# Keys of both branches in three single PSUM banks per tile, and a third row tile transposed on the array

## The chip, the cores and the metric

The kernel runs on one core of a Trainium2 chip. The metric is the device time of one execution in microseconds, and smaller is better.

## The reference

The reference computes two linear-attention branches, A and B, on the same input rows and mixes them with a gate. For `x` of 2048 rows by 640 columns and each branch with its own `wqkv` (640 x 1920) and `wo` (640 x 640):

```
qkv = (x @ wqkv) split into q, k, v with H = 32 heads of 20
phi = lambda t: where(t > 0, t + 1, exp(t)) + 1e-6
pq, pk = phi(q), phi(k)
kv = einsum("bhsd,bhse->bhde", pk, v);   z = einsum("bhsd->bhd", pk)
o  = einsum("bhqd,bhde->bhqe", pq, kv) / (einsum("bhqd,bhd->bhq", pq, z) + 1e-6)
branch = o (heads joined) @ wo
g = sigmoid(sum(x * gate_w))          # one number per row
result = g * branch_A + (1 - g) * branch_B
```

All operands are bfloat16. `phi` is computed as max(t, 0) + (min(exp(t), 1) + 1e-6), which is the same function.

## The kernel before

The 2048 rows are 16 row tiles of 128 (`NT`), and the 640 input columns are five chunks of 128 (`NC`). `XT` holds x transposed (chunk columns on the partitions, rows along the free side), which is the stationary operand of the key products; `XN` holds x as it is.

There are four stages in the order of TensorE. First the keys of both branches for all 16 tiles. Then, for each branch, five sums over all rows of keys times x (`g_unit`, L643 and L644), with the query products (`q_unit`, L797) between them. Then small products for the key-value matrices (L705, whose moving operand takes five runs of 24 columns) and for those times `wo` (L740). Last, the output products (L957), which ScalarE and VectorE bring out of PSUM.

Every operation is recorded by a helper with an estimated cost, the buffers that it reads and writes, and a priority. A planner then runs the list in simulated time. TensorE keeps the order in which its work was recorded; ScalarE (ACT), VectorE (DVE) and SyncE (SP) take the operation that can start earliest. From this come the final order on each engine, the PSUM banks, and the semaphore waits. PSUM is a pool of 8 banks of 512 fp32 columns; a buffer takes one bank, or two neighbouring ones. The loads at the beginning are chained by queue in the order recorded.

The loads go out from SP (L354 in the trace, the helper's line) in this order: x tile 0, then the five weight chunks of A's keys (called A0 to A4 below) and the five of B's (B0 to B4), 160 KB each. Then seven transposing DMAs bring the row tiles 2 to 15 into `XT` (the first four take one tile each), one plain load brings x rows 256 to 2047 into `XN`, and last come the other weights. x tile 1 and the gate weights are issued from ACT's queue.

Tiles 0 and 1 don't wait for transposing DMAs. `x_tp` (L479) multiplies each plain 128 x 128 block of x by the identity `IDN` on TensorE, which transposes it into PSUM, and three copies (L496, one block, two blocks, two blocks) bring it into `XT`: on VectorE for tile 0, on ScalarE for tile 1. While their weights come in, A's keys of tiles 0 and 1 are interleaved chunk by chunk. `gate_col` puts the gate weights into the column after B's key weights (a small matmul at L516 and a copy at L519), so that column 640 of B's key product is the gate's logit.

A key product of one tile and one branch (`k_step`) is five steps, one for each chunk, and each step is a matmul of 512 columns (L535) and one of 128 (A) or 129 columns (B, L536) into a buffer of two PSUM banks. `k_post` then runs: for B a one-column exponential for the gate (L561), an exponential over 640 columns on ACT into a slot of `EK` (L568), a clamp in place on DVE (L571), and the sum with max(t, 0) on DVE, which reads PSUM (L579) and writes the keys `PK`. `EK` has four slots of 640 columns, one for each product. The query exponentials (L814) wait for the last key of branch B, since their slots lie over `EK`.

`warm` (L466) is work for TensorE before data is there. The lines around the start read:

Of the kernel before, what the change touches and what calls it, by code (L numbers as in the profile page):

```python
# [7 lines left out]
ALU = mybir.AluOpType  # L8
# [3 lines left out]
D = 640  # L12
# [64 lines left out]
class Sched:  # L77
# [187 lines left out]
def body(nc, A_x, A_wqkv, A_wo, B_x, B_wqkv, B_wo, gate_w, out, log=None):  # L265
# [9 lines left out]
    XT = sb("XT", [128, NC, S], bf)  # L275
    XN = sb("XN", [128, NT, XS_W], bf)
    WKW = sb("WKW", [128, 2 * NU * D], bf)
    WK = {
        "A": WKW[:, 0 : NC * D].rearrange("p (c f) -> p c f", c=NC),
        "B": WKW[:, NC * D : NC * (D + KB_W)].rearrange("p (c f) -> p c f", c=NC),  # L280
    }
    WQ = {X: sb("WQ" + X, [128, NC, D], bf) for X in XS}
    WV = {X: sb("WV" + X, [128, NC, D + 8], bf) for X in XS}
    WO = {X: sb("WO" + X, [128, NU, D], bf) for X in XS}
    PK = {X: sb("PK" + X, [128, NT * D], bf) for X in XS}
    PKt = {X: PK[X][:, :].rearrange("p (t f) -> p t f", t=NT) for X in XS}
    EX = [sb("EX%d" % i, [128, NC, 512], bf) for i in range(3)]

    def slot(X, i):
# [58 lines left out]
    def dma(q, name, dst, src, nbytes, ins=(), outs=(), after=(), issue=450.0, transpose=False, prio=None):  # L348
        timing = (330.0, 1500.0) if not transpose else (140.0, 1500.0) if loading else (1000.0, 1150.0)

        def fn(e):
            d = dst() if callable(dst) else dst
            with nc.allow_non_contiguous_dma(reason="layout"):
                return e.dma_start(d, src() if callable(src) else src, transpose=transpose)  # L354

        o = op(q, fn, 0.0, ins, outs, after, prio=prio, name=name, dma=(issue, nbytes) + timing)
        if loading:
            o.behind = chain.get(q)
            chain[q] = o
        return o  # L360
# [4 lines left out]
    def act_cost(n):  # L365
        return 190 + 0.833 * n

    def dve1(n):
        return 155 + 1.04 * n
# [34 lines left out]
    def ld_x(q, t):  # L404
        dma(q, "x%d" % t, XN[:, t, 0:D], x[128 * t : 128 * t + 128, :], 163840, outs=[bxn[t]])

    def ld_wk(q, X, c, after=()):
        dma(q, "wk%s%d" % (X, c), WK[X][:, c, 0:D], wqkv[X][128 * c : 128 * c + 128, D : 2 * D], 163840, outs=[bwk[X, c]], after=after)
# [19 lines left out]
    for c in range(NC):  # L428
        if c == 0:
            ld_x("SP", c)  # L430
        ld_wk("SP", "A", c)
    for c in range(NC):
        ld_wk("SP", "B", c)
    for t0, t1 in ((2, 3), (3, 4), (4, 5), (5, 6), (6, 8), (8, 12), (12, 16)):
        xt_dma(t0, t1)
    dma("SP", "xr", XN[:, 2:NT, 0:D], x[256:S, :].rearrange("(t p) d -> p t d", p=128), 14 * 163840, outs=bxn[2:])
    for X in XS:
        dma("SP", "wq" + X, WQ[X][:, :, :], w3(X, 0), 819200, outs=[bwq[X]])
    for X in XS:
# [22 lines left out]
    def warm(n, w=4):  # L462
        for i in range(n):
            op(
                "PE",
                lambda e: e.matmul(psw(bw, 128 * w), ONE[:, 0:1].to_broadcast([128, 128]), ONE[:, 0:1].to_broadcast([128, 128 * w]), start=True, stop=True),  # L466
                107.0 * w,
                ins=[bone],
                outs=[bw],
                name="warm",  # L470
            )

    def x_tp(t):
        for lo, hi in ((0, 1), (1, 3), (3, 5)):
            bt = Buf("tp", "ps")
            for c in range(lo, hi):
                op(
                    "PE",
                    lambda e, c=c, lo=lo, bt=bt: e.matmul(  # L479
                        PS[:, bt.slot, 128 * (c - lo) : 128 * (c - lo) + 128],  # L480
                        XN[:, t, 128 * c : 128 * c + 128],
                        IDN[:, :],
                        start=True,
                        stop=True,
                    ),
                    100.0,
                    ins=[bxn[t], bid],
                    outs=[bt],
                    name="tp%d" % t,
                )  # L490
            half = Buf("xth")

            def copy(e, lo=lo, hi=hi, bt=bt):
                o = XT[:, lo:hi, 128 * t : 128 * t + 128]
                i = PS[:, bt.slot, 0 : 128 * (hi - lo)].rearrange("p (c s) -> p c s", c=hi - lo)
                return e.activation(o, i, ACT.Copy) if t else e.tensor_copy(o, i)  # L496

            op(
                "ACT" if t else "DVE",
                copy,  # L500
                act_cost(128 * (hi - lo)) if t else dve1(128 * (hi - lo)),
                ins=[bt],
                outs=[half],
                name="tpc%d" % t,
            )
            bxt[t].parts = getattr(bxt[t], "parts", []) + [half] * (hi - lo)
# [3 lines left out]
    def gate_col():  # L510
        bt = Buf("gwp", "ps")

        def tv():
            return PS[:, bt.slot, 0:NC]

        op("PE", lambda e: e.matmul(tv(), GWZ[:, :], IDN[:, 0:NC], start=True, stop=True), 60.0, ins=[bgw, bid], outs=[bt], name="gwt")  # L516
        op(
            "DVE",
            lambda e: e.tensor_copy(WK["B"][:, :, D : D + 1], tv().unsqueeze(2)),  # L519
            170.0,  # L520
            ins=[bt],
            outs=[bgc],
            name="gwc",
        )
# [4 lines left out]
    def k_step(X, t, c, ps):  # L529
        w = D + 1 if X == "B" else D  # L530

        def fn(e):
            a = psw(ps, w)
            l = XT[:, c, 128 * t : 128 * t + 128]
            e.matmul(a[:, 0:512], l, WK[X][:, c, 0:512], start=(c == 0), stop=(c == NC - 1))  # L535
            return e.matmul(a[:, 512:w], l, WK[X][:, c, 512:w], start=(c == 0), stop=(c == NC - 1))  # L536

        xin = [bxt[t].parts[c] if hasattr(bxt[t], "parts") else bxt[t]]
        op(
            "PE",  # L540
            fn,
            mm_cost(512) + mm_cost(128),
            ins=xin + [bwk[X, c]] + ([bgc] if X == "B" else []),
            outs=[ps],
            name="k%s%d_%d" % (X, t, c),
        )
# [3 lines left out]
    def k_post(X, t, ps):  # L550
        ek = Buf("ek", "ek")
        ek2 = Buf("ek2")
        pk = Buf("pk%s%d" % (X, t))
        bpk[X, t] = pk
        first = []
        if X == "B":
            b = Buf("ge")
            bge.append(b)
            op(
                "ACT",  # L560
                lambda e: e.activation(GE[:, t : t + 1], psw(ps, D + 1)[:, D : D + 1], ACT.Exp, scale=-1.0),  # L561
                200.0,
                ins=[ps],
                outs=[b],
                name="ge",
            )
            first = [b]
        op("ACT", lambda e: e.activation(EK[:, ek.slot, :], psw(ps, D), ACT.Exp), act_cost(D), ins=[ps] + first, outs=[ek], name="ke")  # L568
        op(
            "DVE",  # L570
            lambda e: e.tensor_scalar(EK[:, ek.slot, :], EK[:, ek.slot, :], 1.0, EPS, op0=ALU.min, op1=ALU.add),  # L571
            dve4(D),
            ins=[ek],
            outs=[ek2],
            name="kt",
        )
        op(
            "DVE",
            lambda e: e.scalar_tensor_tensor(PKt[X][:, t, :], psw(ps, D), 0.0, EK[:, ek.slot, :], op0=ALU.max, op1=ALU.add),  # L579
            dve1(D),  # L580
            ins=[ps, ek, ek2],
            outs=[pk],
            name="ks",
        )

    def k_unit(X, t):
        ps = Buf("k", "ps", 2)
        for c in range(NC):
            k_step(X, t, c, ps)
        k_post(X, t, ps)  # L590

    warm(4)
    warm(1, 2)
    pss = [Buf("k", "ps", 2) for _ in range(2)]
    x_tp(0)
    warm(1, 1)
    x_tp(1)
    for c in range(2):
        for t in range(2):
            k_step("A", t, c, pss[t])  # L600
    gate_col()
    for c in range(2, NC):
        for t in range(2):
            k_step("A", t, c, pss[t])
    for t in range(2):
        k_post("A", t, pss[t])
    pss = [Buf("k", "ps", 2) for _ in range(2)]
    for c in range(NC):
        for t in range(2):
            k_step("B", t, c, pss[t])  # L610
    for t in range(2):
        k_post("B", t, pss[t])
    for t in range(2, NT):
        for X in XS:
            k_unit(X, t)

    LOW = 10**6

# [529 lines left out]
```

## Time and profile before

| | us |
|---|---|
| median of 4 runs | 188.0 |
| lowest, highest | 187.92, 188.52 |
| profiled execution, own time | 188.52 |
| its span, first to last instruction | 186.8 |
| TensorE busy in the span | 183.4 |
| ScalarE busy | 94.8 |
| VectorE busy | 136.9 |

The profiled execution is the slowest of the four runs, and its span leaves 1.72 us that lie around the instructions. The TensorE clock was granted in full (1.000) over the whole span.

Busy time of the engines in stretches of the span, in us:

| stretch | work of TensorE | PE | DVE | ACT |
|---|---|---|---|---|
| 0 to 7.65 | first loads, transposes, A's keys of tiles 0 and 1 | 6.37 | 1.21 | 2.43 |
| 7.65 to 48.6 | all other keys | 40.95 | 34.21 | 24.00 |
| 48.6 to 100 | sums over rows, queries | 51.40 | 31.96 | 28.66 |
| 100 to 150 | the rest of them, small products, first outputs | 49.99 | 46.79 | 31.19 |
| 150 to 186.8 | outputs | 34.73 | 22.68 | 8.55 |

A line for a group of instructions names the source line, the engine, the operation, what is written from what, the shape and the count; then the busy time of all, the printed nanoseconds of one, and the time in which the engine sat idle ahead of them with what ended it. Matmuls overlap in the pipeline, so the printed length of one is longer than the distance from its start to the next one's. PEld is the loading of the stationary operand, which runs beside the matmuls. A line of a timeline gives the start, the length, the engine, the source line and the operation.

### The profile page before, as it was taken

How to read it: one execution, taken by the hardware profiler on the slowest of the kernel's cores; microseconds unless marked ns; L12 is line 12 of the kernel's file. 1: busy time of each engine (PE TensorE's matmuls, PEld its weight loads, DVE VectorE, ACT ScalarE, POOL GpSimd, SP SyncE). 2: the span in 40 equal slices, each digit the busy share in tenths (PEclk: the TensorE clock that was granted, in tenths of full speed). 3: DMA queues.
4: the chain of work that ended last, by engine and by line, in shares of the span. 5: the costliest groups of instructions: out<-in, count | busy, mean ns of one | idle time of the engine just before them, and what ended most of it. 6: DMA issues, size and time to landing. Idle time of an engine off the chain costs nothing.

```text
span 186.8 us, 3272 instructions
## 1 busy us (share of the span) xinstructions
PE 183.4 (98%) x1297; PEld 106.6 (57%) x1297; DVE 136.9 (73%) x264; ACT 94.8 (51%) x167; POOL 0.8 (0%) x10
## 2 busy tenths in 40 slices
PE   8899999999999999999999999999999999999995
PEld 4455555555555655555557555555567555555553
DVE  2289888888833455487699999998799996359653
ACT  5265655656454546544675566788623784400001
POOL 1000000000000000000000000000000000000000
PEclk9999999999999999999999999999999999999999
DMA  7989999997001011010611312116515346613434
GB/s 193 290 156 142 211 387 368 364 213 154 4 0 35 0 39 35 0 35 10 85 28 35 74 28 51 28 41 174 177 35 115 64 100 168 171 70 108 142 106 140
DMA packets 36501, 21.38 MB, mean 114 GB/s; under 512 B 25694, under 2 KB 36230, under 8 KB 36486
## 3 DMA queue, kind: packets, MB, share of 16 engines
q1 hardware_dynamic: 36188, 20.97, 45.1%
q8 instruction: 10, 0.16, 0.4%
q10 hardware_dynamic: 298, 0.20, 0.3%
q14 instruction: 5, 0.04, 0.1%
HBM read 10.87 MB, written 4.26 MB: 81 GB/s over the span
## 4 chain that ended last, share of the span: by engine, by line
PE 96%; DMA 2%; SPq 1%; DVE 0%; issue 0%; DVEq 0%
PE ps L957 23%; PE ps L797 23%; PE ps L643 18%; PE ps L535 18%; PE ps L644 5%; PE ps L536 5%; DMA WKW<-in_A_wqkv_dram 2%; PE ps L705 2%; PE ps L740 1%; SPq L354 1%; DVE TSB L1001 0%; DVEq L237 0%
## 5 line engine op out<-in xcount | busy, mean ns | idle before, releaser
L535 PE MATMUL ps<-WKW,XT 128*128 128x512 bf16 x160 | 43.9, 380 | 0.8 <-DMA WKW<-in_A_wqkv_dram 0.8
L814 ACT ACTIVATE EK<-ps 128x512 bf16<-128x512 f32 x40 | 23.9, 598 | 30.7 <-PE ps L797 30.6
L536 PE MATMUL ps<-WKW,XT 128*128 128x128 bf16 (+1 forms) x160 | 35.1, 220 | 0.0
L568 ACT ACTIVATE EK<-ps 128x640 bf16<-128x640 f32 x32 | 22.3, 704 | 10.4 <-PE ps L536 5.0
L535 PEld LDWEIGHTS ps<-WKW,XT 128*128 128x128 bf16 x160 | 15.7, 98 | 19.8 <-DMA WKW<-in_A_wqkv_dram 1.2
L797 PE MATMUL ps<-XT,WQA 128*128 128x512 bf16 x100 | 24.5, 379 | 0.0
L797 PE MATMUL ps<-XT,WQB 128*128 128x512 bf16 x100 | 23.8, 380 | 0.0
L643 PE MATMUL ps<-XN,PKB 128*128 128x512 bf16 x80 | 23.5, 379 | 0.0
L643 PE MATMUL ps<-XN,PKA 128*128 128x512 bf16 x80 | 23.5, 379 | 0.0
L824 DVE TENSOR_SCALAR EK<-EK 128x512 bf16<-128x512 bf16 x40 | 11.5, 288 | 13.7 <-ACT EK L814 13.7
L644 PE MATMUL ps<-XN,PKA 128*128 128x129 bf16 x80 | 17.6, 220 | 0.0
L644 PE MATMUL ps<-XN,PKB 128*128 128x129 bf16 x80 | 17.6, 220 | 0.0
L957 PE MATMUL ps<-WPA,EX 128*128 128x512 bf16 x120 | 17.0, 299 | 0.0
L957 PE MATMUL ps<-WPB,PKA 128*128 128x512 bf16 x120 | 16.5, 299 | 0.0
L797 PEld LDWEIGHTS ps<-XT,WQB 128*128 128x128 bf16 x100 | 10.9, 118 | 8.8 <-issue 0.4
L571 DVE TENSOR_SCALAR EK<-EK 128x640 bf16<-128x640 bf16 x32 | 10.4, 325 | 7.4 <-ACT EK L568 7.3
L536 PEld LDWEIGHTS ps<-WKW,XT 128*128 128x128 bf16 x160 | 15.7, 98 | 0.0
L797 PEld LDWEIGHTS ps<-XT,WQA 128*128 128x128 bf16 x100 | 10.6, 117 | 8.1
L643 PEld LDWEIGHTS ps<-XN,PKA 128*128 128x128 bf16 x80 | 9.4, 117 | 7.9
L643 PEld LDWEIGHTS ps<-XN,PKB 128*128 128x128 bf16 x80 | 9.4, 117 | 7.9
L579 DVE SCALAR_TENSOR_TENSOR PKB<-ps,EK 128x640 bf16<-128x640 f32 x16 | 13.2, 825 | 0.6
L579 DVE SCALAR_TENSOR_TENSOR PKA<-ps,EK 128x640 bf16<-128x640 f32 x16 | 13.2, 825 | 0.6
(77 smaller groups left out, 222.3 us busy)
## 6 DMA issues: line engine op xcount, KB each, us to landing
out_dram<-TSB SPq DMA_DIRECT2D x15, 160.0 KB, 1.8
XN<-in_A_x_dram SPq DMA_DIRECT2D x1, 2240.0 KB, 9.2
WKW<-in_A_wqkv_dram SPq DMA_DIRECT2D x5, 160.0 KB, 4.4
WKW<-in_B_wqkv_dram SPq DMA_DIRECT2D x5, 160.0 KB, 4.3
WQA<-in_A_wqkv_dram SPq DMA_DIRECT2D x1, 800.0 KB, 10.8
WQB<-in_B_wqkv_dram SPq DMA_DIRECT2D x1, 800.0 KB, 13.4
WVA<-in_A_wqkv_dram SPq DMA_DIRECT2D x1, 800.0 KB, 12.7
WVB<-in_B_wqkv_dram SPq DMA_DIRECT2D x1, 800.0 KB, 14.4
```

Of the source, the lines that this page charges most:

```text
L535: e.matmul(a[:, 0:512], l, WK[X][:, c, 0:512], start=(c == 0), stop=(c == NC - 1))
L536: return e.matmul(a[:, 512:w], l, WK[X][:, c, 512:w], start=(c == 0), stop=(c == NC - 1))
L568: op("ACT", lambda e: e.activation(EK[:, ek.slot, :], psw(ps, D), ACT.Exp), act_cost(D), ins=[ps] + first, outs=[ek], name="ke")
L571: lambda e: e.tensor_scalar(EK[:, ek.slot, :], EK[:, ek.slot, :], 1.0, EPS, op0=ALU.min, op1=ALU.add),
L579: lambda e: e.scalar_tensor_tensor(PKt[X][:, t, :], psw(ps, D), 0.0, EK[:, ek.slot, :], op0=ALU.max, op1=ALU.add),
L643: e.matmul(a[:, 0:512], l, XN[:, t, 0:512], start=(t == 0), stop=(t == NT - 1))
L644: return e.matmul(a[:, 512 : D + 1], l, XN[:, t, 512 : D + 1], start=(t == 0), stop=(t == NT - 1))
L705: r = e.matmul(PS[0:n, ps.slot, GR * i : GR * i + NC * w], WV[X][:, c, lo : lo + n], gv[:, c, :, 24 * u : 24 * u + w], start=(c == 0), sto ...
L797: r = e.matmul(PS[:, ps.slot, :], WQ[X][:, c, g::5], XT[:, c, 512 * b : 512 * b + 512], start=(c == 0), stop=(c == NC - 1),)
L814: lambda e: e.activation(EQ[:, eq.slot, :], PS[:, ps.slot, :], ACT.Exp),
L824: lambda e: e.tensor_scalar(EQ[:, eq.slot, :], EQ[:, eq.slot, :], 1.0, EPS, op0=ALU.min, op1=ALU.add),
L957: r = e.matmul(a[:, l0 - lo : h0 - lo], PQ[X, b][:, g, 128 * (t % 4) : 128 * (t % 4) + 128], WP[X][:, g, l0:h0], start=(X == first and g = ...
```

## The change

Two things change, both in the key stage.

The head: row tile 2 is no longer brought by a transposing DMA. It is loaded plainly, from SP after the first A weight chunk, and transposed on TensorE by `x_tp(2)` with its three copies on VectorE. The bulk load into `XN` begins at row 384. A's keys of tiles 0, 1 and 2 are then interleaved as the weights come in, and B's keys of these three tiles follow tile by tile with `k_unit`.

From tile 3 on, a new function `k_both` takes the place of the two `k_unit` calls. The 640 + 640 key columns and the gate column of one tile are computed as three products in single banks: 512 columns of A, then 258 columns (129 of A and 129 of B in one matmul, whose moving operand is two runs), then 512 columns of B. The weights of both branches lie beside each other in `WKC` for this, and the gate column is written behind both. The exponentials, clamps and sums follow the banks: exponentials of 512, 256 and 512 columns and the gate's one, one clamp over 768 columns and one over 512, sums of 512, 256 and 512. `EK` serves as two pairs of slots, one pair for a tile. `PK` of both branches is one tensor now, so that one sum can write both.

```diff
+    WKC = WKW[:, 0 : NC * 2 * KB_W].rearrange("p (c x f) -> p c x f", c=NC, x=2)
+    WK = {X: WKC[:, :, i, :] for i, X in enumerate(XS)}
...
+    PKS = sb("PKS", [128, 2, NT * D], bf)
+    PK = {X: PKS[:, i, :] for i, X in enumerate(XS)}
...
         ld_wk("SP", "A", c)
+        if c == 0:
+            ld_x("SP", 2)
     for c in range(NC):
         ld_wk("SP", "B", c)
-    for t0, t1 in ((2, 3), (3, 4), (4, 5), (5, 6), (6, 8), (8, 12), (12, 16)):
+    for t0, t1 in ((3, 4), (4, 5), (5, 6), (6, 8), (8, 12), (12, 16)):
         xt_dma(t0, t1)
...
-                "ACT" if t else "DVE",
+                "ACT" if t == 1 else "DVE",
                 copy,
...
-            lambda e: e.tensor_copy(WK["B"][:, :, D : D + 1], tv().unsqueeze(2)),
+            lambda e: e.tensor_copy(WKC[:, :, :, D : D + 1], tv().unsqueeze(2).unsqueeze(3).to_broadcast([128, NC, 2, 1])),
...
+    def k_both(t):
+
+        ps = [Buf("k", "ps") for _ in range(3)]
+        ek = Buf("ek", "ek", 2, (0, 2))
...
+        for i in range(3):
+
+            def fn(e, i=i):
+                for c in range(NC):
+                    r = WKC[:, c, :, 512 : D + 1] if i == 1 else WKC[:, c, i // 2, 0:512]
+                    x = e.matmul(two() if i == 1 else bank(i), XT[:, c, 128 * t : 128 * t + 128], r, start=(c == 0), stop=(c == NC - 1))
+                return x
...
+        op("ACT", lambda e: e.activation(ekw(0, 512), bank(0), ACT.Exp), act_cost(512), ins=[ps[0]], outs=[ek, ea], name="ke")
+        op("ACT", lambda e: e.activation(GE[:, t : t + 1], two()[:, 0, D - 512 : D - 511], ACT.Exp, scale=-1.0), 200.0, ins=[ps[1]], outs=[b], name="ge")
+        op(
+            "ACT",
+            lambda e: e.activation(ekw(512, 768).rearrange("p (x f) -> p x f", x=2), two()[:, :, 0:128], ACT.Exp),
...
+        clamp(0, 768, [ea, em], ta)
+        add(PKt["A"][:, t, 0:512], lambda: bank(0), lambda: ekw(0, 512), 0, [ta], [pk["A"]])
+        add(
+            PKS[:, :, D * t + 512 : D * t + D],
...
+        op("ACT", lambda e: e.activation(ekw(768, 1280), bank(2), ACT.Exp), act_cost(512), ins=[ps[2]], outs=[ek, eb], name="ke")
+        clamp(768, 1280, [eb], tb)
+        add(PKt["B"][:, t, 0:512], lambda: bank(2), lambda: ekw(768, 1280), 2, [tb], [pk["B"]])
...
     warm(1, 1)
     x_tp(1)
+    for t in range(2):
+        k_step("A", t, 0, pss[t])
+    x_tp(2)
+    for t in range(2):
+        k_step("A", t, 1, pss[t])
     for c in range(2):
-        for t in range(2):
-            k_step("A", t, c, pss[t])
+        k_step("A", 2, c, pss[2])
     gate_col()
-    for c in range(2, NC):
+    for c in range(2, 4):
         for t in range(2):
             k_step("A", t, c, pss[t])
     for t in range(2):
+        k_step("A", t, 4, pss[t])
         k_post("A", t, pss[t])
...
+    for c in range(2, NC):
+        k_step("A", 2, c, pss[2])
+    k_post("A", 2, pss[2])
+    for t in range(3):
+        k_unit("B", t)
+    for t in range(3, NT):
+        k_both(t)
```

More of the change, by code (lines that the diff above doesn't have):

```diff
@@ L277, in body @@
     WKW = sb("WKW", [128, 2 * NU * D], bf)
[L278 to L281, printed above, removed]
+    WKC = WKW[:, 0 : NC * 2 * KB_W].rearrange("p (c x f) -> p c x f", c=NC, x=2)
+    WK = {X: WKC[:, :, i, :] for i, X in enumerate(XS)}
     WQ = {X: sb("WQ" + X, [128, NC, D], bf) for X in XS}
@@ L284, in body @@
     WO = {X: sb("WO" + X, [128, NU, D], bf) for X in XS}
-    PK = {X: sb("PK" + X, [128, NT * D], bf) for X in XS}
-    PKt = {X: PK[X][:, :].rearrange("p (t f) -> p t f", t=NT) for X in XS}
+    PKS = sb("PKS", [128, 2, NT * D], bf)
+    PK = {X: PKS[:, i, :] for i, X in enumerate(XS)}
+    PKt = {X: PK[X].rearrange("p (t f) -> p t f", t=NT) for X in XS}
     EX = [sb("EX%d" % i, [128, NC, 512], bf) for i in range(3)]
@@ L431, in body @@
         ld_wk("SP", "A", c)
+        if c == 0:
+            ld_x("SP", 2)
     for c in range(NC):
         ld_wk("SP", "B", c)
-    for t0, t1 in ((2, 3), (3, 4), (4, 5), (5, 6), (6, 8), (8, 12), (12, 16)):
+    for t0, t1 in ((3, 4), (4, 5), (5, 6), (6, 8), (8, 12), (12, 16)):
         xt_dma(t0, t1)
-    dma("SP", "xr", XN[:, 2:NT, 0:D], x[256:S, :].rearrange("(t p) d -> p t d", p=128), 14 * 163840, outs=bxn[2:])
+    dma("SP", "xr", XN[:, 3:NT, 0:D], x[384:S, :].rearrange("(t p) d -> p t d", p=128), 13 * 163840, outs=bxn[3:])
     for X in XS:
@@ L495, in copy @@
                 i = PS[:, bt.slot, 0 : 128 * (hi - lo)].rearrange("p (c s) -> p c s", c=hi - lo)
-                return e.activation(o, i, ACT.Copy) if t else e.tensor_copy(o, i)
+                return e.activation(o, i, ACT.Copy) if t == 1 else e.tensor_copy(o, i)
             op(
-                "ACT" if t else "DVE",
+                "ACT" if t == 1 else "DVE",
                 copy,
-                act_cost(128 * (hi - lo)) if t else dve1(128 * (hi - lo)),
+                act_cost(128 * (hi - lo)) if t == 1 else dve1(128 * (hi - lo)),
                 ins=[bt],
@@ L590, in k_unit, with bank, two, ekw @@
         k_post(X, t, ps)
+    def k_both(t):
+        ps = [Buf("k", "ps") for _ in range(3)]
+        ek = Buf("ek", "ek", 2, (0, 2))
+        pk = {X: Buf("pk%s%d" % (X, t)) for X in XS}
+        b, ea, em, eb, ta, tb = [Buf("kq") for _ in range(6)]
+        def bank(i, w=512):
+            return PS[:, ps[i].slot, 0:w]
+        def two():
+            return bank(1, 2 * (D - 511)).rearrange("p (x f) -> p x f", x=2)
+        def ekw(lo, hi):
+            return EK[:, ek.slot : ek.slot + 2, :].rearrange("p k f -> p (k f)")[:, lo:hi]
+        for i in range(3):
[5 more added lines that the diff above has]
+            op(
+                "PE",
+                fn,
+                NC * mm_cost((512, 258, 512)[i]),
+                ins=[bxt[t], bgc] + list(bwk.values()),
+                outs=[ps[i]],
+                name="kk%d_%d" % (t, i),
+            )
+        bpk["A", t], bpk["B", t] = pk["A"], pk["B"]
+        bge.append(b)
+        op("ACT", lambda e: e.activation(ekw(0, 512), bank(0), ACT.Exp), act_cost(512), ins=[ps[0]], outs=[ek, ea], name="ke")
+        op("ACT", lambda e: e.activation(GE[:, t : t + 1], two()[:, 0, D - 512 : D - 511], ACT.Exp, scale=-1.0), 200.0, ins=[ps[1]], outs=[b], name="ge")
+        op(
+            "ACT",
+            lambda e: e.activation(ekw(512, 768).rearrange("p (x f) -> p x f", x=2), two()[:, :, 0:128], ACT.Exp),
+            act_cost(256),
+            ins=[ps[1], b],
+            outs=[ek, em],
+            name="ke",
+        )
+        def clamp(lo, hi, ins, out):
+            op(
+                "DVE",
+                lambda e: e.tensor_scalar(ekw(lo, hi), ekw(lo, hi), 1.0, EPS, op0=ALU.min, op1=ALU.add),
+                dve4(hi - lo),
+                ins=ins,
+                outs=[out],
+                name="kt",
+            )
+        def add(dst, src, e1, i, ins, outs):
+            op(
+                "DVE",
+                lambda e: e.scalar_tensor_tensor(dst, src(), 0.0, e1(), op0=ALU.max, op1=ALU.add),
+                dve1((512, 256, 512)[i]),
+                ins=[ps[i], ek] + ins,
+                outs=outs,
+                name="ks",
+            )
+        clamp(0, 768, [ea, em], ta)
+        add(PKt["A"][:, t, 0:512], lambda: bank(0), lambda: ekw(0, 512), 0, [ta], [pk["A"]])
+        add(
+            PKS[:, :, D * t + 512 : D * t + D],
+            lambda: two()[:, :, 0:128],
+            lambda: ekw(512, 768).rearrange("p (x f) -> p x f", x=2),
+            1,
+            [ta],
+            [pk["A"], pk["B"]],
+        )
+        op("ACT", lambda e: e.activation(ekw(768, 1280), bank(2), ACT.Exp), act_cost(512), ins=[ps[2]], outs=[ek, eb], name="ke")
+        clamp(768, 1280, [eb], tb)
+        add(PKt["B"][:, t, 0:512], lambda: bank(2), lambda: ekw(768, 1280), 2, [tb], [pk["B"]])
@@ L592, in body @@
     warm(4)
     warm(1, 2)
-    pss = [Buf("k", "ps", 2) for _ in range(2)]
+    pss = [Buf("k", "ps", 2) for _ in range(3)]
     x_tp(0)
@@ L605, in body @@
     for t in range(2):
+        k_step("A", t, 4, pss[t])
         k_post("A", t, pss[t])
[L607 to L615, printed above, removed]
+    for c in range(2, NC):
[5 more added lines that the diff above has]
+        k_both(t)
     LOW = 10**6
```

## The prediction

> **What bounds the kernel now.** I read the page's busy shares first, then the slices, then the chain of waits.
>
> ```profile
> PE 183.4 (98%) x1297; PEld 106.6 (57%) x1297; DVE 136.9 (73%) x264; ACT 94.8 (51%) x167; POOL 0.8 (0%) x10
> ...
> PE 96%; DMA 2%; SPq 1%; DVE 0%; issue 0%; DVEq 0%
> ...
> L536 PE MATMUL ps<-WKW,XT 128*128 128x128 bf16 (+1 forms) x160 | 35.1, 220 | 0.0
> L568 ACT ACTIVATE EK<-ps 128x640 bf16<-128x640 f32 x32 | 22.3, 704 | 10.4 <-PE ps L536 5.0
> ...
> L571 DVE TENSOR_SCALAR EK<-EK 128x640 bf16<-128x640 bf16 x32 | 10.4, 325 | 7.4 <-ACT EK L568 7.3
> ```
>
> TensorE is on 96% of the chain that ends last, ScalarE and VectorE wait for it, and its key matmuls have no idle time before them. So a microsecond is worth something only where TensorE works or waits. Its waits over the whole span, from the waits of PE and of its weight loads, are few, and those of this stage lie in the first 6 us:
>
> ```profile
> PE ps L535 <- DMA WKW<-in_A_wqkv_dram: 0.8, 2, 0.5
> ...
> PEld ps L535 <- DMA WKW<-in_A_wqkv_dram: 1.2, 2, 0.8
> ```
>
> The timeline of PE shows both, and the gate matmul between them:
>
> ```profile
> 4.28 0.22 PE L536 MATMUL ps<-WKW,XT 128*128 128x128 bf16 x1
> 5.01 0.39 PE L535 MATMUL ps<-WKW,XT 128*128 128x512 bf16 x1 [0.51 <-DMA WKW<-in_A_wqkv_dram]
> ...
> 5.56 0.17 PE L516 MATMUL ps<-IDN,GWZ 128*128 128x5 bf16 x1
> 6.01 0.39 PE L535 MATMUL ps<-WKW,XT 128*128 128x512 bf16 x1 [0.28 <-DMA WKW<-in_A_wqkv_dram]
> ...
> 7.65 0.38 PE L535 MATMUL ps<-WKW,XT 128*128 128x512 bf16 x1
> ...
> 48.47 0.38 PE L643 MATMUL ps<-XN,PKA 128*128 128x512 bf16 x1
> 49.56 1.24 PE L797 MATMUL ps<-XT,WQA 128*128 128x512 bf16 x5
> 50.64 0.38 PE L643 MATMUL ps<-XN,PKA 128*128 128x512 bf16 x1
> ```
>
> The key stage of branch B begins at 7.65 and the next stage at 48.47. In between lie 150 pairs (512 and 128 or 129 columns): 40.82 / 150 = 0.2721 us a pair. The printed 380 and 220 ns overlap; only distances between starts add up. A query unit, five matmuls of 512, takes 50.64 - 49.56 = 1.08, 0.216 each. So a 512 costs 0.216 and the short one 0.056.
>
> **What the Trainium skill says.** "TensorE: Matmul & The Clock Gate", section "Wait — 56ns, not 53.3ns?", gives a warm matmul as N / 2.4 GHz plus about 2.5 ns. The trace agrees: 512 / 2.4 = 213.3 against 216, and 128.5 / 2.4 = 53.5 against 56. "DMA: Bandwidth & Descriptors", section "Issuing engines are not separate DMA queues", says that DMAs from every queue end on the same 16 engines and interleave. The windows agree that these are full early: a DMA share of 1.00 at 5 to 6 us, with 341 GB/s. "PSUM — Partial Sum Buffer", section "Specifications (TRN2)", warns that any non-contiguous access pattern slows matmuls significantly; the one strided moving operand in this trace (L705, five runs of 24 columns) doesn't show it: 30 of 120 columns in 1.53 us of the chain, 51 ns each.
>
> **The change part by part.**
>
> *Matmul count.* For each of 13 tiles, ten pairs (10 x 512, 5 x 128, 5 x 129) become 10 x 512 and 5 x 258. Five matmuls fewer save 5 x 2.6 = 13 ns, and A's unneeded gate column adds 5 x 0.42 = 2 ns: 11 ns a tile, 0.14 us in all, on the path. The moving operand of the 258 has one jump (two runs of 129). By L705 a jump costs nothing; I take 0.110 us. The bound below is the plain sum, the bound above a second fixed cost at the jump, 65 x 2.6 ns = 0.17 us, which just eats the saving. The page's "significantly" would be more: a rival.
>
> *Head, tile 2.* SP issues x tile 2 after the first A weight chunk, so every later SP DMA of this region, A1 to A4, B0 to B4, is issued one place later. The TensorE then does five more transposes, DVE three more copies.
>
> ```profile
> 0.45 2.31 SPq L354 DMA_DIRECT2D WKW<-in_A_wqkv_dram  x5
> 2.80 2.34 SPq L354 DMA_DIRECT2D WKW<-in_B_wqkv_dram  x5
> 5.18 14.93 SPq L354 DMA_TRANSPOSE XT<-in_A_x_dram  x7
> ```
>
> And one piece of the chain of waits, start and length, the third weight chunk (A2) from the end of its issue to its landing:
>
> ```profile
> 1.38 4.58 DMA WKW<-in_A_wqkv_dram
> ```
>
> The first lines (SP's timeline) give the issues. The weight chunks are issued 0.47 us apart, and 164 KB per 0.47 us is 349 GB/s, about the 341 that the engines move when full. So I treat the landings as slots in the order of issue. In before the slot issued at 0.91 (A1) lands near 4.96 and that of 1.38 (A2) at 5.96. In after x2 gets the first and A1 the second. A2 to A4 follow with the lag of 4.4 us that the median of the A chunks shows: 6.3, 6.7, 7.2.
>
> PE then: c0 of tiles 0 and 1 ends at 4.34 as now. It waits for x2 to 4.96 and does five transposes. The 128-column matmul on a warm array costs 0.056, so 0.28 us; the ones of x_tp(1), on a slower array, took 0.53 (3.19 to 3.72). Either ends by 5.5, inside the wait for A1, so they cost nothing; if A1 came earlier they would cost their 0.28 to 0.53. A1 lands at L = 5.96, the pair starts 0.05 later (as 5.96 to 6.01 now). From there 13 pairs of A remain (2 of c1 for tiles 0 and 1, 2 of tile 2, 9 others) and the gate matmul, 0.05: 13 x 0.272 + 0.05 + 0.05 = 3.64. A1 to A4 are then in time (A2 is wanted at 7.15). A for three tiles ends at L + 3.64 = 9.60. Now the same work, two tiles to 7.65 and five pairs of tile 2, ends at 7.65 + 1.36 = 9.01. Head: +0.59 us, in general L - 5.37. If the extra DMA only pushes A1 by one issue, 4.96 + 0.47 = 5.43, the head costs 0.06.
>
> *What hides the copies and banks.* The three DVE copies take 0.29 + 0.41 + 0.41 (L496), and finish near 6.3; tile 2's first pair is due at 6.55. Its two banks come from those that held the transposes, so 0.25 us of cover; beyond it each late 0.1 is paid in full. B's four last weights land near 9.4, B tile 0 starts at 9.6 and needs its fifth chunk at 10.7.
>
> *Tile 3 onward.* One transposing DMA goes away, so xt3, issued at 6.45 or so now, leaves near 5.65; it is wanted at 13.7. All later loads move forward about 0.8 us on SP, and none is waited for now. Worth nothing.
>
> *ScalarE and VectorE.* ACT per tile: 512, gate, 256, 512. From 704 ns for 640 and 598 for 512, 0.83 ns an element: 0.60 + 0.26 + 0.39 + 0.60 = 1.85 us, of 2.71 for PE. DVE starts now: clamp to add 0.36, add to next 0.79. After: clamp 768 0.40 (325 against 288 ns gives 0.29 an element), adds 0.66, 0.40, 0.66, clamp 0.32: 2.44 us, against 2.30 now. That is 90% of PE's rate: VectorE stays behind TensorE but doesn't set it. Bank use: a tile's first bank is freed about 3.5 us after the tile starts, the middle 3.9, the last 4.9; held times 3.5, 2.8, 3.3 sum to 9.6, divided by 2.71 are 3.5 banks of 8. EK has two pairs of slots, so it holds two tiles: a tile's pair is free at 4.9 and wanted again at 6.7. No stall; cover 1.8 us.
>
> *Seam to the next stage.* The last add of the tile ends 2.15 us after PE leaves it, 50.13 + 0.82 - 48.47 = 2.48 now. The query exponentials, which wait for it, start no later relative to PE. From there on everything shifts with PE.
>
> Sum: +0.59 - 0.14 = +0.45 us. The profiled execution was 188.52 us, its span 186.8 plus 1.72 around it, and would be 188.97. It is the slowest of four; on the median of 188.0 I forecast 188.45. Under 0.3% (0.56 us) can't be told from no change here.
>
> **The rivals.**
>
> *1. Harmless head* (forecast's other side of L). x2 is a solid block of rows, and x0 landed 2.5 us and x1 2.8 after issue, against 4.3 for the weights. If x2 lands by 4.3, its transposes fill today's gap, and A1 at 5.43 or earlier brings 187.9; with both waits (0.51 + 0.28) closed, the transposes still paid (0.28) and 0.14 saved, the best is 187.35. Against it: the engines are busy 0.85 to 1.00 between 2 and 6 us, so bytes placed ahead of A1 must delay it.
>
> *2. Head worse, slower than before.* Place: the first pair of A1 or of tile 2 at 6 us. Price: one for one beyond L = 6.07, where head minus saving passes 0.56. A1 at 6.4 gives 188.0 + 1.03 - 0.14 = 188.9. For it: A2's 1.0 us step after A1 shows uneven landings, and the bank cover is only 0.25. Against: the B chunks, with the most ahead of them, lag no more than 4.3 at the median.
>
> *3. Key stage slower.* The 258 pays for its jump (at 0.160 instead of 0.110, 65 x 0.05 = 3.2 us: 191.7), or VectorE passes PE's rate (from 2.71 a tile it eats cover, about 3.0 on it stalls PE). L705 speaks against the first, 0.27 us spare a tile against the second. A new order of ACT, DVE and SP from the planner, since costs differ, can move either sign later, where DVE is busy 46.8 of 50 us (100 to 150).
>
> **How the numbers follow.** Forecast (L 5.4 to 6.07) 0.46, 187.9 to 188.56; harmless head 0.13, half of it below -0.3%; head worse 0.27, 188.6 to 189.3; key stage or order 0.14, mostly slower. No change takes 0.46 + 0.06; slower 0.27 + 0.13; faster 0.07 + 0.01. The range from 187.7 to 189.3 leaves out the best case and the jump.
>
> **What would show it.** The head: a wait of PE on x2, five transposes, then on A1 up to about 6; B's first pair at 9.6. Key stage: 2.71 us between tiles, 258s at 0.110 distance, no PE idle, DVE near 2.44 a tile. Start of the next stage at 48.92 instead of 48.47. Wrong if A1 lands outside 5.4 to 6.07, if PE waits on PSUM banks, if the 258s are more than 0.115 apart, or if the distance from stage start to the end (186.8 - 48.47 = 138.3) changes by more than 0.2.

## The result and the profile after

The changed kernel takes 188.44 us (median of 38 runs, 187.85 to 189.29), the kernel before 188.0 (59 runs, 187.46 to 188.79). The ratio is 1.0022, with an interval from 1.0014 to 1.0031: slower by 0.2%, and under the 0.3% below which the prediction called it no change. The profiled execution took 188.99 us, 187.6 of them span, and is again one of the longer ones of its kernel.

The page of the changed kernel, busy shares and the chain of waits by engine:

```profile
PE 183.8 (98%) x1237; PEld 105.9 (56%) x1237; DVE 138.0 (74%) x280; ACT 96.6 (52%) x180; POOL 0.8 (0%) x10
...
PE 93%; DMA 5%; SPq 1%; DVE 1%; issue 0%; DVEq 0%
```

TensorE bounds it as before, but the DMA share of the chain rose from 2 to 5%. The timeline of TensorE (start, length, then the instruction):

```profile
4.88 0.45 PE L480 MATMUL ps<-IDN,XN 128*128 128x128 bf16 x5
5.97 0.39 PE L536 MATMUL ps<-WKW,XT 128*128 128x512 bf16 x1 [0.63 <-DMA WKW<-in_A_wqkv_dram]
...
9.53 0.38 PE L536 MATMUL ps<-WKW,XT 128*128 128x512 bf16 x1
...
13.62 2.66 PE L614 MATMUL ps<-WKW,XT 128*128 128x512 bf16 x14
...
48.88 0.38 PE L726 MATMUL ps<-XN,PKS 128*128 128x512 bf16 x1
```

Read it against the prediction: x tile 2's five transposes at 4.88 (4.96 expected), the first pair of A1 at 5.97 (6.01), branch B at 9.53 (9.60), the next stage at 48.88 (48.92). The 13 tiles of the new function fill 13.62 to 48.88: 35.26 / 13 = 2.712 us a tile, against 2.721 for ten pairs before. Taking 0.216 for each of the ten 512s leaves 0.110 for a 258. The groups of the key stage (busy time, mean ns):

```profile
L614 PE MATMUL ps<-WKW,XT 128*128 128x258 bf16 x65 | 9.3, 273 | 0.0
L651 DVE SCALAR_TENSOR_TENSOR PKS<-ps,EK 128x256 bf16<-128x256 f32 x13 | 5.4, 414 | 0.0
L641 DVE TENSOR_SCALAR EK<-EK 128x768 bf16<-128x768 bf16 x13 | 4.7, 360 | 4.1 <-ACT EK L631 4.1
```

No idle time stands before the matmuls of the new function, so no PSUM bank came late, and VectorE still waits for ScalarE, 0.37 us in each of 11 of the 13 tiles (L641): it doesn't set the pace.

The surprise is at the end. The waits of the changed kernel:

```profile
DVE TSB L1084 <- DMA out_dram<-TSB: 1.5, 1, 1.5
...
PEld ps L536 <- DMA WKW<-in_A_wqkv_dram: 0.8, 1, 0.8
...
PE ps L536 <- DMA WKW<-in_A_wqkv_dram: 0.6, 1, 0.6
...
DVE DNT L975 <- DMA TTR<-TSH: 0.2, 1, 0.2
```

and the end of its chain:

```profile
181.55 4.14 DMA out_dram<-TSB
185.69 0.02 issue
185.71 0.29 DVE TSB L1084
```

The last copy (128 columns, L1001 before, L1084 after) writes output slot 0, which the output three tiles earlier still holds. That output's DMA took 4.14 us, where the median of the 15 full outputs is 1.8. TensorE was done such that the copy could have started near 185.05 (184.84 before, plus the 0.21 by which the last TensorE work is later). So 0.66 us of this execution's time is a wait of which the prediction has nothing.

Two waits that the prediction didn't look at are in the profile before:

```profile
DVE DNT L892 <- DMA TTR<-TSH: 1.5, 1, 1.5
...
PEld ps L797 <- DVE KVLA L685: 0.3, 1, 0.3
```

VectorE waited for a transposing DMA until 92.43, got behind, and near 104 TensorE lost 0.2 us: the profile puts its wait down to a VectorE operation (L685) that empties a PSUM bank. After the change this wait is gone. From the start of the next stage to the last matmul group it is 135.62 us in both profiles of the changed kernel, against 135.82 and 135.73 in the two of the kernel before.

### The profile page after: what moved, and what is told of

Read it like the earlier page. It is cut to its first block, busy times and chain, and to the rows that moved or that the text cites. A ratio compares the mean times of both kernels' runs of the same rounds, so it can differ in the third digit from the quotient of the medians.

```text
span 187.6 us, 3155 instructions
## 1 busy us (share of the span) xinstructions
PE 183.8 (98%) x1237; PEld 105.9 (56%) x1237; DVE 138.0 (74%) x280; ACT 96.6 (52%) x180; POOL 0.8 (0%) x10
## 4 chain that ended last, share of the span: by engine, by line
PE 93%; DMA 5%; SPq 1%; DVE 1%; issue 0%; DVEq 0%
PE ps L880 23%; PE ps L1040 21%; PE ps L614 19%; PE ps L726 18%; PE ps L727 5%; PE ps L536 3%; DMA WKW<-in_A_wqkv_dram 2%; DMA out_dram<-TSB 2%; PE ps L788 2%; PE ps L823 1%; PE ps L537 1%; SPq L353 1%; DVE TSB L1077 0%; DVE TSB L1084 0%; DVEq L237 0%
## 5 line engine op out<-in xcount | busy, mean ns | idle before, releaser
L726 PE MATMUL ps<-XN,PKS 128*128 128x512 bf16 x160 | 46.9, 379 | 0.0
L897 ACT ACTIVATE EK<-ps 128x512 bf16<-128x512 f32 x40 | 23.9, 598 | 30.2 <-PE ps L880 30.2
L614 PE MATMUL ps<-WKW,XT 128*128 128x512 bf16 (+1 forms) x195 | 35.4, 343 | 0.0
L727 PE MATMUL ps<-XN,PKS 128*128 128x129 bf16 x160 | 35.2, 220 | 0.0
L614 PEld LDWEIGHTS ps<-WKW,XT 128*128 128x128 bf16 x195 | 18.9, 97 | 16.2
L726 PEld LDWEIGHTS ps<-XN,PKS 128*128 128x128 bf16 x160 | 18.8, 117 | 15.8
L651 DVE SCALAR_TENSOR_TENSOR PKS<-ps,EK 128x512 bf16<-128x512 f32 (+1 forms) x39 | 22.3, 599 | 0.9
L727 PEld LDWEIGHTS ps<-XN,PKS 128*128 128x128 bf16 x160 | 18.8, 117 | 3.1
L1040 PE MATMUL ps<-WPB,PKS 128*128 128x512 bf16 x120 | 16.5, 299 | 0.0
L1040 PEld LDWEIGHTS ps<-WPB,PKS 128*128 128x128 bf16 x120 | 9.3, 98 | 7.2
L904 ACT ACTIVATE PKS<-ps 128x512 bf16<-128x512 f32 x20 | 11.9, 594 | 0.0
L641 DVE TENSOR_SCALAR EK<-EK 128x768 bf16<-128x768 bf16 (+1 forms) x26 | 8.4, 322 | 4.1 <-ACT EK L631 4.1
L668 ACT ACTIVATE EK<-ps 128x512 bf16<-128x512 f32 x13 | 7.8, 597 | 6.4 <-PE ps L614 6.4
L627 ACT ACTIVATE EK<-ps 128x512 bf16<-128x512 f32 x13 | 7.8, 597 | 6.1 <-PE ps L614 5.8
```

The costliest lines, as they stand in the source:

```text
L614: x = e.matmul(two() if i == 1 else bank(i), XT[:, c, 128 * t : 128 * t + 128], r, start=(c == 0), stop=(c == NC - 1))
L627: op("ACT", lambda e: e.activation(ekw(0, 512), bank(0), ACT.Exp), act_cost(512), ins=[ps[0]], outs=[ek, ea], name="ke")
L641: lambda e: e.tensor_scalar(ekw(lo, hi), ekw(lo, hi), 1.0, EPS, op0=ALU.min, op1=ALU.add),
L651: lambda e: e.scalar_tensor_tensor(dst, src(), 0.0, e1(), op0=ALU.max, op1=ALU.add),
L668: op("ACT", lambda e: e.activation(ekw(768, 1280), bank(2), ACT.Exp), act_cost(512), ins=[ps[2]], outs=[ek, eb], name="ke")
L726: e.matmul(a[:, 0:512], l, XN[:, t, 0:512], start=(t == 0), stop=(t == NT - 1))
```

## The experiments

Twelve runs follow, two of them repeats of the kernels before and after. Every edit is shown against the changed kernel. Theories: (1) the recorded one, the load of x tile 2 costs some 0.5 us and the banks give 0.14 back; (2) the head is harmless and the banks cost; (3) everything sits in the wait at the end; later (4) the landings at the start vary from execution to execution and (5) an instruction fetch makes the late landing at the end. Ratios are to the kernel before on the same chip.

### One part at a time

The head alone, and once more:

```diff
     for t in range(3, NT):
-        k_both(t)
+        for X in XS:
+            k_unit(X, t)
```

> The head of the change alone; from tile 3 on the keys are computed per branch as before. Theory 1 (the plain x tile 2, one place ahead of the second A weight chunk, costs some 0.5 us, and the banks give back 0.14): A1 lands near 5.9, branch B starts near 9.5, the next stage near 49.0 instead of 48.47 (before) and 48.88 (change), and the time is 188.0 + 0.5 = 188.5. Theory 2 (the head is harmless and the single-bank keys, or the copies behind them, cost the 0.44): next stage 48.5, 188.0. Theory 3 (the whole difference sits at the end, in the last copy's wait for a late output DMA): 188.0, and the wait doesn't depend on the head.

> The head alone once more, since its six runs (189.56) lie above both kernels it stands between. Theory 4 (head varies, head costs about 1 us on average, the single banks give back 0.6): 189.0 to 189.5. If the six runs were drawn from a bad chip visit: 188.5, the sum of the prediction's own steps.

The single banks alone, with the head of before (two tiles transposed on the array, tile 2 by transposing DMA):

```diff
-        if c == 0:
-            ld_x("SP", 2)
-    for t0, t1 in ((3, 4), (4, 5), (5, 6), (6, 8), (8, 12), (12, 16)):
+    for t0, t1 in ((2, 3), (3, 4), (4, 5), (5, 6), (6, 8), (8, 12), (12, 16)):
...
-    for t in range(3, NT):
+    for t in range(2, NT):
         k_both(t)
```

> The single-bank keys alone, from tile 2 on, with the head of before (tile 2 by transposing DMA). Theory 1: 14 tiles save 11 ns each, 0.15 us, next stage at 48.3, time 187.85. Theory 2: the single banks cost the 0.44, next stage 48.9, time 188.4. Theory 3: next stage 48.3, but the wait of the last copy at the end is there and the time is 188.2 or more.

The head alone: 189.56 us, ratio 1.0091 [1.0066, 1.0116], six runs; again 189.34, 1.0074 [1.0059, 1.0089]. The banks alone: 187.37, ratio 0.9978 [0.9963, 0.9993]. So theory 2 has the signs wrong, and theory 1 has them right and both sizes too small: the head alone costs 1.4 to 1.7 us, the banks give 0.4 by the ratio and 0.6 by the medians. Together that would be some +1.0, and the change costs 0.44: the two parts don't add up, so something besides them changes from kernel to kernel.

The head's profiles show that not all of this is head. The next stage starts at 48.58 and 48.52, between the two profiles of the changed kernel (48.88, and 48.12 further down), but TensorE's last work is followed by 3.3 us instead of 2.5. The DMAs of the head alone in its last 4 us (a packet of instructions, then outputs with size and time to landing):

```profile
q14 instruction: 1, 0.01, 0.8%
...
out_dram<-TSB SPq DMA_DIRECT2D x1, 128.0 KB, 2.5
out_dram<-TSB ACTq DMA_DIRECT2D x1, 32.0 KB, 2.4
```

The last two outputs land in 2.5 and 2.4 us, in both profiles, where before they took 1.7 and 1.6, and a fetch of instructions lies in the same stretch. The kernel before has such a fetch in its second profile, but after 186, when its outputs have landed. That is 0.8 us at the end of the span, far behind x tile 2 and its weights. That this fetch causes it isn't shown: elsewhere fetches of this size (queue q14, 0.01 MB) leave the outputs beside them at 1.8, as at 176 to 178 us in the changed kernel.

### Where the head's cost comes from

x tile 2 issued from ACT's queue, so that SP issues A1 at its old time; and the cost doubled, with a second plain load (x tile 3) ahead of A1:

```diff
     ld_x("ACT", 1)
+    ld_x("ACT", 2)
...
-        if c == 0:
-            ld_x("SP", 2)
```

> The changed kernel with the load of x tile 2 issued from ACT's queue behind x tile 1, so that SP issues A1 at 0.91 as before. If the bytes ahead of A1 delay it (theory 1), A1 still lands near 5.9 and the time stays 188.4; if only the later place in SP's order does, A1 lands near 4.96, TensorE waits little, branch B starts near 9.0 and the time is 187.9.

```diff
             ld_x("SP", 2)
+            ld_x("SP", 3)
```

> The changed kernel with a second plain load ahead of A1 (x tile 3, which then is left out of the bulk load; its transposing DMA stays): the suspected cost doubled. Theory 1: A1 moves by one more slot of 0.4 to 0.5 us, to about 6.35, every later start with it, and the time is 188.85. Theory 2 and 3: no change from 188.4, as TensorE's head isn't what counts.

From ACT's queue: 187.91 us, ratio 1.0005 [0.9988, 1.0021]. Its TensorE timeline:

```profile
4.32 0.44 PE L479 MATMUL ps<-IDN,XN 128*128 128x128 bf16 x5
4.69 0.39 PE L535 MATMUL ps<-WKW,XT 128*128 128x512 bf16 x1
```

The transposes begin at 4.32 and A1's first pair follows at once: A1 had landed by then, although the same bytes of x tile 2 were asked for ahead of it (ACT issues both tiles from 0.12 to 0.99, SP issues A1 at 0.92). It landed 3.7 us after its issue; in the four profiles with the old head that lag is 3.4 to 4.1. The next stage starts at 47.61; 0.6 us of that are lost again at the last copy. This speaks for the time at which SP issues A1 and against the bytes ahead of it, though it is one profile, and its ratio's interval overlaps with that of the changed kernel.

Two loads ahead: 188.42, ratio 1.0027 [1.0015, 1.0039], no more than the changed kernel, where 188.85 was expected. SP issues A1 at 1.86, and TensorE's timeline has:

```profile
5.86 0.61 PE L537 MATMUL ps<-WKW,XT 128*128 128x512 bf16 x1 [0.30 <-DMA WKW<-in_A_wqkv_dram]
...
6.37 0.49 PE L537 MATMUL ps<-WKW,XT 128*128 128x512 bf16 x1
...
6.75 0.38 PE L537 MATMUL ps<-WKW,XT 128*128 128x512 bf16 x1
```

A1's first pair starts at 5.86, not at the 6.35 of theory 1, and within the 5.08 to 5.97 of the kernels with one load ahead. The next stage at 49.12 is the latest of all, but 0.35 us of that isn't a landing: the pairs for A1 start 0.51 and 0.38 us apart instead of 0.27, because the array is still slow here. So this one profile can't tell two loads from one, and the median shows nothing of the second.

The kernel before, unchanged, for a second profile, and the changed kernel likewise:

> The kernel before, unchanged, for a second profile of it. In the first, the second and third A weight chunks were waited for until 4.96 and 5.96; the run with the single banks alone has the same loads and landed them at 4.7 and before 5.3. If the landings vary from execution to execution (theory 4), branch B starts here at another time than 7.65, between 6.9 and 7.7, and the next stage 40.8 later; everything from there to the last output product keeps its distances within 0.2 us. If the first profile was typical (theory 1 as predicted), B starts at 7.6 to 7.7.

> The changed kernel unchanged, for a second profile and for times beside the others of this call: 188.2 to 188.5, the wait of the last copy there again, the second A weight chunk between 5.0 and 5.9, and everything from the next stage's start to the last output product at the same distances to 0.02 us.

Before, second profile (187.53 us), TensorE:

```profile
4.58 0.38 PE L535 MATMUL ps<-WKW,XT 128*128 128x512 bf16 x1
...
5.31 0.39 PE L535 MATMUL ps<-WKW,XT 128*128 128x512 bf16 x1
...
6.95 0.38 PE L535 MATMUL ps<-WKW,XT 128*128 128x512 bf16 x1
```

A1's first pair at 4.58 (5.01 in the first profile), A2's at 5.31 (6.01), B at 6.95 instead of 7.65. The profile that the prediction was made from had weights that landed late, by 0.7 us at the start of B. After, second profile (187.83 us; the median of the 22 runs beside it is 188.32, ratio 1.0020 [1.0009, 1.0031]):

```profile
5.20 0.39 PE L536 MATMUL ps<-WKW,XT 128*128 128x512 bf16 x1
...
48.12 0.38 PE L726 MATMUL ps<-XN,PKS 128*128 128x512 bf16 x1
```

A1's first pair at 5.20, not 5.97. Over the profiles with A1 issued from SP and at most x tile 2 ahead of it, the start of the next stage is:

| kernels with the old head | us | kernels with x tile 2 on SP ahead of A1 | us |
|---|---|---|---|
| before | 48.47, 47.77 | changed | 48.88, 48.12 |
| banks alone | 47.79 | changed, six slots; own slot; more waits | 48.00, 48.09, 48.58 |
| banks, six slots | 47.98 | head alone | 48.58, 48.52 |

Taking 0.14 off the pairs' kernels (before, head alone) to stand them beside the others, the means are 47.93 and 48.36. The head costs 0.43 us on average in these profiles, with a standard error of some 0.2, and with a spread of 0.7 us between executions of one kernel.

So the start varies, but theory 4 is only half of it. The landings vary, as A1 and A2 show above. So does the time at which the array gets fast: pairs start 0.53 us apart at first and 0.27 later. In the changed kernel with six slots the second pair of all already follows after 0.32 (3.76, 4.08). In the banks alone with six slots three pairs in a row take 0.53 (3.68, 4.21, 4.74, 5.28), and branch B starts at 7.28, although A1 landed sooner there than in any other profile of the old head, 3.4 us after its issue.

### The end

Six output slots for four, with the banks alone and with the change:

```diff
-    NEK, NEQ, NOS = 4, 4, 4
+    NEK, NEQ, NOS = 4, 4, 6
```

> The single banks with the head of before, and six output slots instead of four, so that the last copy doesn't reuse the slot of a DMA that is just leaving. Order of all instructions as in the run with four slots. If a late output DMA in the last 6 us makes the upper group of times (188.0 to 188.2 against 187.1 to 187.7), that group goes and the median falls to about 187.3; if the head makes it, both groups stay.

> The changed kernel with six output slots. Late output DMA as the cause of the upper group (188.7 to 189.3): it goes, median about 188.2, and the last copy waits for TensorE alone. Head as the cause: 188.4 and both groups.

187.51, ratio 0.9981 [0.9972, 0.9990], and 187.95, ratio 0.9997 [0.9985, 1.0010]. This was a poor experiment: the planner still gave the last copy slot 0, three outputs after it was last used, and in the second kernel the copy waited for a DMA of 4.1 us as before. The upper times did not go (187.14 to 188.27 with the banks alone). It serves as a second measurement of the banks. The second kernel lies 0.4 to 0.5 us under the changed kernel at other times; whether the six slots or the occasion does that is open.

The two that do touch the wait: a place of its own for the last copy, and 44 more instructions on TensorE (waits already fulfilled) to move its instruction fetch:

```diff
-        os_, bo = Buf("os", "os"), Buf("ob")
+        os_, bo = Buf("os", "ol" if eng == "DVE" else "os"), Buf("ob")
...
-            op("DVE", lambda e: e.tensor_copy(OST[:, os_.slot, 0:w], psw(ps, w)), dve1(w), ins=[ps], outs=[os_], name="oc")
+            op("DVE", lambda e: e.tensor_copy(TSB[:, 3968 : 3968 + w], psw(ps, w)), dve1(w), ins=[ps], outs=[os_], name="oc")
```

> The changed kernel, the last 128-column copy in columns of its own instead of output slot 0, which the output three tiles earlier still holds (six slots left it in slot 0). Order of instructions unchanged. Theory 5 (an instruction fetch near 182 us makes that output DMA land 2 us late, and the copy waits for it): the copy starts 0.6 us sooner, right behind TensorE, and the time is 0.3 to 0.6 us under the changed kernel of the same call. If the wait is only something that shows beside another limit: no difference.

```diff
+AGAIN = tuple("qA%d%d" % (b, g) for b in (1, 2, 3) for g in range(5))
...
             for d in o.keep:
-                eng.wait_ge(d.sem, d.count)
+                for _ in range(8 if o.name in AGAIN else 1):
+                    eng.wait_ge(d.sem, d.count)
```

> The changed kernel with 44 more instructions on TensorE, repeated waits on semaphores that have already been reached, in the query units of branch A. They hold up nothing if TensorE's queue covers them. Theory 5: TensorE's instruction fetch follows the count of its instructions, so the last one comes some 3 us earlier, near 179; the output DMA of slot 0 lands in 1.8 us again, the last copy doesn't wait, and the time is 0.3 to 0.6 us under the changed kernel of the same call. If the late landing has nothing to do with the fetch, it stays where it was, near 182, and so does the time.

DMAs of the changed kernel between 180 and 184 us, then of the one with moved instructions, between 177 and 181 and between 180 and 184 (queue, packets, MB, share of 16 engines; outputs with their median time to landing):

```profile
q8 instruction: 1, 0.02, 1.5%
...
out_dram<-TSB SPq DMA_DIRECT2D x3, 160.0 KB, 3.2
```

```profile
q8 instruction: 1, 0.02, 2.7%
...
out_dram<-TSB SPq DMA_DIRECT2D x3, 160.0 KB, 3.1
...
out_dram<-TSB SPq DMA_DIRECT2D x4, 160.0 KB, 1.9
```

Queue q8 carries TensorE's instructions, since more of them on TensorE moved its fetch: from between 183.25 and 183.5 us to between 179.5 and 179.75. The slow landings went with it: 3.1 in its stretch, 1.9 in the later one. In none of the profiles with the old head and the single banks is there such a fetch after 166, and all their outputs issued after that land in 1.9 or less. In all fourteen profiles, the outputs of 160 KB that are under way during a fetch on q8 or leave soon after it land in 2.0 to 4.1, and the others in 1.8 or 1.9. That the fetch makes the outputs late is shown. What it is worth in the median is not. The last copy in the changed kernel's second profile, in the one with its own place, and in the one with moved instructions:

```profile
184.55 0.29 DVE L1084 CAST TSB<-ps 128x128 bf16<-128x128 f32 x1 [1.08 <-DMA out_dram<-TSB]
```

```profile
184.19 0.29 DVE L1084 CAST TSB<-ps 128x128 bf16<-128x128 f32 x1 [0.74 <-PE ps L1040]
```

```profile
184.75 0.29 DVE L1086 CAST TSB<-ps 128x128 bf16<-128x128 f32 x1 [0.81 <-PE ps L1042]
```

In the last two the wait is TensorE's again, and the times are 188.15 with its own place, ratio 1.0003 [0.9993, 1.0013], and 188.34 with moved instructions, ratio 1.0026 [1.0014, 1.0038], against 188.32 of the changed kernel beside them. The first falls by 0.17, with intervals that overlap, the second not at all, with eight runs. The 0.3 to 0.6 that theory 5 asked for was not there. Within a profile the wait counts in full: from the start of the next stage to the end of the span it is 138.7 us in the three profiles in which the last copy loses 0.6 to 0.7, 138.3 in the one in which it loses 0.27, and 138.2 in the three kernels with the new head and the single banks in which it loses nothing. But it is 0.66 in one execution of the changed kernel and 0.27 in the next, and its share in the median stays open. Theory 3, that the end is all, falls too.

### The banks alone, once more

The banks alone is some 0.2% faster than the kernel before in both forms above. One more, with A1 issued from ACT's queue and left out of SP's:

```diff
     ld_x("ACT", 1)
+    ld_wk("ACT", "A", 1)
...
-        ld_wk("SP", "A", c)
...
+        if c != 1:
+            ld_wk("SP", "A", c)
```

> The single banks with the head of before, and A1 issued from ACT's queue behind x tile 1, so that A2 to A4 and B move up one place on SP. If the order of issue sets the landings: TensorE's waits in the first 6 us go, branch B starts near 6.8 and the time is 0.1 to 0.3 under 187.4 to 187.5. If the bytes set them: no change.

187.51 us, ratio 0.9979 [0.9966, 0.9992]. TensorE no longer waits for A1, but for A2, until 5.34; B starts at 6.98 and nothing is gained over the banks alone, where 0.1 to 0.3 was expected.

## Why the prediction was right

The forecast was 188.45 and the time is 188.44. The signs of both its terms are confirmed, and the saving of the banks in the key stage as it was worked out. The working of the head was not right, three terms that it has not nearly cancel, and so the closeness of the sum is luck.

*Matmul count.* Predicted 11 ns a tile, 0.14 us. Measured 9 ns a tile, 0.12 us. A 258 costs 0.110 as taken: the jump in its moving operand costs nothing that shows, and the third rival's 0.160 is out. The warning on access patterns that the prediction quotes is one about PSUM. The 258 writes one run there, and its two runs lie in SBUF, so neither it nor L705 tests that warning.

*Head.* Predicted +0.59, by the first profile's slots. The changed kernel's first profile gives +0.52 at branch B (9.53 against 9.01), the average of the profiles +0.43. The size held, its working did not. The prediction moved A1 by a whole slot, from 4.96 to 5.96; the runs show a landing 3.6 to 4.5 us after the issue (3.4 to 4.1 with the old head), and an issue that is 0.47 later, so A1's first pair starts between 5.08 and 5.97 in seven profiles with the new head, 5.49 in the middle, and between 4.58 and 5.01 in four with the old one. In three of the seven A1 landed by 5.2, under the 5.4 at which the prediction called itself wrong. And it measured that against a start of B at 7.65 which was itself late (6.95, 6.97 and 7.28 in three other profiles of the same head). Both readings come from the same late execution and are wrong by nearly the same amount, so their difference survived. Its other value, A1 pushed by one issue to 5.43, was nearer to what the profiles show on average, but set against the late start it gave only 0.06.

*Bytes ahead of A1* (the argument against the first rival, that they must delay it): not borne out. With the same bytes issued from another queue, A1 wasn't delayed in the one profile taken. SP's 0.47 us of issue is the cost that shows. A1's first pair moves by 0.68 on average, though, and its lag is 4.0 with the new head against 3.7 with the old; whether the rest is bytes or spread, these runs don't settle.

*Copies and banks in the head.* The three copies of tile 2 lay between 5.15 and 6.10, before tile 2's first pair at 6.52 needed them. They cost nothing, and nor did tile 2's PSUM banks.

*ScalarE and VectorE.* 2.44 us of VectorE a tile was expected. The starts of its tiles are 2.71 us apart, like TensorE's, with 0.37 us of waiting for ScalarE, so it needed 2.34. Right, and a little on the safe side.

*The rest keeps its distances.* The step that failed. Predicted: from the next stage to the end 138.3 us, wrong beyond 0.2. Measured 138.7 in the first profile, and 138.3 in the second. Inside the first lie a gain of 0.2 (TensorE no longer waits near 104) and the loss of 0.66 at the last copy; in the second the loss is 0.27, and the two cancel. Around the span the two profiled executions differ by 0.33 us (1.72 and 1.39), which the prediction took as fixed; the medians over the runs are 1.53 to 1.59 for the kernel before and 1.36 to 1.38 for the changed one. Why it is shorter is open.

So the median's +0.44 is, as far as the runs go: head +0.43, banks -0.12, wait near 104 -0.1 to -0.2, around the span -0.15 to -0.2, and what is left, +0.4 to +0.5, at the end. The last figure is the remainder of the sum and not a measurement; removing the wait gave 0.17 at most.

## What to carry to other kernels

Before reading a landing time out of one profile of a few-microsecond head, take a second: here the third weight chunk landed 0.7 us apart in two executions, which is more than the change is worth, and the array got fast at different times too. A small load put ahead of others delays them at least by the issue time of its queue, 0.47 us here; another queue that is free may issue it for less, as one profile showed here. When two edits are measured separately at the level of a few tenths of a per cent, look at the end of the profile as well: a changed number of instructions moves the fetches of instructions, and these can make an output late.

## What the runs showed of the hardware

Fetches of instructions share the DMA engines with data. TensorE's stream is fetched in pieces of 0.02 MB (ten in the changed kernel's 187.6 us, on q8), and a fetch of 1.5% of 16 engines' time in 4 us is 0.96 us of one engine's (0.015 x 16 x 4). Outputs of 160 KB that are under way beside one land in 2.0 to 4.1 us instead of 1.8 or 1.9. The Trainium skill says, in "DMA: Bandwidth & Descriptors", section "Queues, rings and completion order", that each DMA engine takes turns between queues a packet at a time, and in "Why a DMA increments its semaphore by 16 and not by 1", that a DMA's semaphore counts up to 16 engines that finish independently; that fits a DMA held up by its slowest engine, though it doesn't give the 2 us.

From the start of the second stage to VectorE's last sum over 640 columns lie 134.53 us, the same to 0.01 in all ten profiles with the single banks; with the keys computed by pairs it is 134.64 to 135.00. So the 134 us in the middle repeat almost exactly, and what varies between executions of one kernel lies in the head, before branch B, and in the last 4 us.
